# Attention and a two-layer network on one core: the product with the spread reciprocals half as far again behind, and later raw scores in the phases that turn sums

## The chip, the cores and the metric

The kernel runs on one NeuronCore of a Trainium2 chip. The metric is the device time of one execution in microseconds; the time before is the median of three runs. All times are us unless marked ns. PE is the matrix engine (PEld its weight loads), DVE the vector engine, ACT the scalar engine, POOL and SP the two engines that here issue nearly all transfers.

## The reference

Two branches on the same rows, mixed by a gate. Branch a is attention with 32 query heads of width 16 over one shared key and value head; branch b is a two-layer network with a squared ReLU.

```python
g = _sigmoid((x * gate_w).sum(-1, keepdims=True))
...
q = (lambda x, *d: x.transpose(*d))((x @ wq).reshape(B, S, H, Dh), 0, 2, 1, 3)
k = x @ wk
v = x @ wv
scores = jnp.einsum("bhqd,bkd->bhqk", q, k) * (Dh ** -0.5)
p = _softmax(scores, axis=-1)
o = jnp.einsum("bhqk,bkd->bhqd", p, v)
return (lambda x, *d: x.transpose(*d))(o, 0, 2, 1, 3).reshape(B, S, H * Dh) @ wo
...
h = jnp.einsum("bsd,df->bsf", x, w1) + b1
r = jnp.where(h > zero, h, zero)
h = r * r
out = jnp.einsum("bsf,fd->bsd", h, w2) + b2
...
return g * a + (1 - g) * b
```

The arrays are float32, with S 2048, D 512, H 32, Dh 16 and F 1792.

## The kernel before

The queries come in 4 chunks of 512 rows, each with 8 groups of 4 heads. For a group, the scores are made for 16 blocks of 128 keys, in two halves of the queries: 1024 units in all. A unit is four heads by 256 queries for one block of keys: two score matmuls of 512 columns (rows 0 to 63 and 64 to 127 of PE work at once), one exponential of 1024 columns on ACT (line 873), and four context matmuls by the values (line 893) that add into the bank acc. The values carry a column of ones, so that the rows of acc hold sums of exponentials beside the outputs.

PE takes turns. A phase (`phase`, line 1236) makes the scores of 4 to 9 units a few units ahead, mixed with the matmuls M of another piece of work (a span: a query projection, a hidden block of the network, a sum by w2, a projection by wo), and then the context matmuls of units made earlier follow (`context`, line 879). The order in a phase is written out by hand in `PLANS`, by the number of units, of matmuls and the kind of the phase: `S0` is a pair of score matmuls into a bank pair s, which ACT reads itself; `02` and `12` are the two halves of unit 2, which go as raw scores through the single bank x. DVE copies each half out of x (line 857), and ACT takes the exponential from the copy. So PE's next use of x waits for DVE's copy. The second part of a plan is the order of the exponentials. The same bank x also serves, now and then, to sum the squares of queries (line 425), and in the last phases to turn sums by PE (`turn`, line 966, the transposes in line 976), from which DVE reads in lines 981 to 985. A list `late` marks that x was just used in that way by the queries' squares; then a phase of 6 units and 12 matmuls, whole, takes the plan `LATER`, whose raw score comes later.

Engines work through their own queues in order. In which order DVE gets its work is decided while the program is written, by a running estimate of each engine's clock (`at_pe`, `at_dve`, `at_act`): `spend` (line 674) fills the gaps before a raw score is due with waiting jobs: remainders of rounded weights, the list `divisions`, biases, and the list `chores`, which loads and rounds the output weights and the attention outputs (lines 643 and 646; L643 is a cast, L646 its remainder).

After two groups of heads, `finish` (line 929) moves sums and outputs by SP into the tiles lq and oc, and `divide` (line 910) makes the jobs of `divisions`, 15 times: clamp the sums (lines 921, 922), invert them and let POOL send them to memory and back, spread over the rows, into lc (line 916, and the transfers in lines 917 and 918), and multiply oc by lc (line 925). `LAST_OK` is 15, and the number i of the division runs from 0 to 14. A job carries an earliest time: the product's is 24 us (`SPREADS`) behind that of the inversion, 10 us for the last one. Then POOL stores the tile (line 959), and when all tiles of a chunk are stored, `ask` (line 1048) puts its loading and rounding on `chores`, from which the chunk's projection by wo follows.

POOL's queue also holds stores of the rounded weights for reuse (line 521) and, in the first part of the program, stores of the queries' remainders (line 369, 15 of them), whose tiles are later taken over by the hidden block's results (lines 202 and 203).

Of the kernel before, what the change touches and what calls it, by code (L numbers as in the profile page):

```python
# [15 lines left out]
OP = mybir.AluOpType  # L16
# [16 lines left out]
ROOT = float(0x1fbd1df5 + 0x80000)  # L33
WARM = 10
LW = 4 * CH // 64
LANDS, DIVIDES, WRITES, SPREADS, SURE = 6.0, 22.0, 14.0, 24.0, 1.4
PAIR, CONTEXT, TURN, EXP, COPY, LATE = 0.235, 0.429, 0.36, 0.925, 0.66, 0.3
GROUPS = [[(0, 1, 2, 3), (4, 5, 6, 7, 8), (9, 10, 11, 12, 13)]] + [[(0, 1, 2, 3, 4), (5, 6, 7, 8, 9), (10, 11, 12, 13)]] * 3
AHEAD = 4
WHOLE, FIRST, SECOND, LATER = range(4)  # L40
# [7 lines left out]
    (6, 12, WHOLE): ("M 02 S0 M S1 M M M M M S3 M M M S4 12 M M S5", (0, 1, 3, 4, 5, 2)),  # L48
    (6, 12, LATER): ("S0 M M S1 M M M 02 M S3 M M M S4 M 12 M M S5", (0, 1, 3, 4, 5, 2)),
    (6, 9, WHOLE): ("S0 M 03 M S1 M M M S2 M M M S4 13 M S5", (0, 1, 2, 4, 5, 3)),  # L50
    (6, 6, WHOLE): ("S0 M S1 M 03 M S2 M 13 M S4 M S5", (0, 1, 2, 4, 3, 5)),
    (6, 6, SECOND): ("S0 M S1 M 03 M S2 M 13 M S4 M S5", (0, 1, 2, 4, 3, 5)),
    (4, 6, WHOLE): ("M 02 S0 M M S1 M M 12 M S3", (0, 1, 3, 2)),
# [9 lines left out]
LAST_OK = NC * KT - 1  # L63
# [106 lines left out]
def mix_kernel(ctx: ExitStack, tc: tile.TileContext, xT, wkv, wq, wo, w12, b1, b2, cst, out):  # L170
    nc = tc.nc
# [66 lines left out]
    with fast, tc.tile_pool(name="at", bufs=1) as at, \  # L238
# [8 lines left out]
        def aside():  # L247
            return mp.tile([128, CH], F32, name="x", bufs=1)
# [420 lines left out]
        def step_aside():  # L669

            if side and next(side[0], "end") == "end":
                side.pop(0)
# [138 lines left out]
        es, wide = {}, []  # L811
# [98 lines left out]
        def divide(o, l, i, ready):  # L910

            n = at.tile([128, LW], F32, name="n")
            wide = at.tile([128, CH], F32, name="lc", bufs=2)

            def over():
                nc.vector.reciprocal(n, n)
                nc.gpsimd.dma_start(ls[i].rearrange("a (b n) -> (a b) n", b=16), n)
                nc.gpsimd.dma_start(wide, bass.AP(tensor=ls.tensor, offset=ls[i].offset,
                                                  ap=[[CH, 8], [0, 16], [1, CH]]))

            return ((0.1, ready, lambda: nc.vector.tensor_scalar(n, l, L_MIN, L_MAX, op0=OP.max, op1=OP.min)),
                    (0.2, ready, lambda: nc.vector.scalar_tensor_tensor(l, n, 1.0, l, op0=OP.mult, op1=OP.is_equal,
                                                                        accum_out=ok[:, i:i + 1])),
                    (0.3, ready, over),
                    (0.72, ready + (SPREADS if i < LAST_OK - 1 else LANDS + 4.0), lambda: nc.vector.tensor_tensor(o, o, wide, OP.mult)))

        sums = []

# [37 lines left out]
        def turn(a, u, js, okc, idle=0):  # L966

            if not o2:
                o2.append(at.tile([128, 4, 2, 4, DH], F32, name="o2", tag="oc", bufs=2))
            js = slice(js[0], js[-1] + 1)  # L970
            m = js.stop - js.start
            if m > 2:
                yield
            tp = aside().rearrange("p (j n) -> p j n", j=4)
            for j in range(m):
                nc.tensor.transpose(tp[:, j], a[:, j * 128:(j + 1) * 128], ident)
            busy(idle)
            p5 = tp[:, :m].rearrange("p j (h d e) -> p j h d e", h=4, e=2)
            l = p5[:, :, :, 0, 1]
            n = at.tile([128, 2, 4, 4], F32, name="nl")[:, :, :m]  # L980
            nc.vector.tensor_scalar(n[:, 0], l, L_MIN, L_MAX, op0=OP.max, op1=OP.min)
            nc.vector.scalar_tensor_tensor(n[:, 1], n[:, 0], 1.0, l, op0=OP.mult, op1=OP.is_equal,
                                           accum_out=ok[:, okc:okc + 1])
            nc.vector.reciprocal(n[:, 0], n[:, 0])
            nc.vector.tensor_tensor(o2[0][:, js, u], p5[:, :, :, :, 0],
                                    n[:, 0].unsqueeze(3).to_broadcast([128, m, 4, DH]), OP.mult)
# [36 lines left out]
        def busy(n):  # L1023

            if n and not junk:
                junk.append(sp.tile([128, 2, CH], F32, name="s")[:, 0])
            for _ in range(n):
                nc.tensor.matmul(junk[0], cs[:, :64].bitcast(BF), cs[:, :CH // 2].bitcast(BF), start=True, stop=True)
# [207 lines left out]
        def phase(slots, n, m):  # L1236

            nonlocal scored, evicted, at_pe
            if span.done[0] == 0:
                begin()  # L1240
            step_aside()
            kind = SECOND if span.done[0] else WHOLE if slots == span.slots else FIRST
            if late and (n, slots, kind) == (6, 12, WHOLE):
                kind = LATER
            late.clear()
            text, order = PLANS.get((n, slots, kind)) or plain(n, slots)
            rows = [], []
            for item in text.split():
                if item[0] == "0":
                    rows[0].append(item)  # L1250
                elif item[0] == "1":
                    rows[1].append(item)
                else:
                    for r in range(2):
                        rows[r].append(item)
            todo = [scored + i for i in order]

            for i in range(len(rows[0])):
                for r in range(2):
                    item = rows[r][i]  # L1260
                    if item == "M":
                        span.product(r)
                    elif item[0] == "S":
                        score_part(scored + int(item[1:]), r)
                    else:
                        score_copy(scored + int(item[1:]), r)
                    exps(todo)
                at_pe += PAIR
            exps(todo)
            assert not todo  # L1270
            scored += n
            if not span.left():
                evicted = span.before
                if evicted:
                    spend(at_pe + 0.3)
                    dve(0.76, at_pe + 0.3)
                    evicted.unit[1](evicted.bank)
            if not any(item[0] == "0" for item in text.split()):
                spend(at_pe)
            while wanted:  # L1280
                w_load(wanted.pop(0))
            for half in range(2):
                if NF <= len(ws[half]) < min(room[half], NC * NF):
                    w_fetch(half)
            for half in halves():
                if spans > 5 and w_ready(half):
                    if at_act + 0.64 < at_pe + 0.7 + CONTEXT * m:
                        w_round(half, scalar_copy)
                    elif at_dve + 0.6 < at_pe + 0.7 + CONTEXT * m:
                        w_round(half, nc.vector.tensor_copy)  # L1290
# [47 lines left out]
        late, halved, units_left = [], [0.0], [NC * (NF + 12) + 15 + 16]  # L1338
# [11 lines left out]
        while u < total:  # L1350
# [6 lines left out]
            m, slots = block(u)  # L1357
# [59 lines left out]
```

## Time and profile before

| what | us |
|---|---|
| median of three runs (lowest, highest) | 1208.13 (1207.78, 1211.83) |
| the profiled execution | 1204.39 |
| its span, first to last instruction | 1202.6 |
| PE busy | 1180.2 |
| ACT busy | 1025.7 |
| DVE busy | 673.0 |
| mean granted PE clock | 0.994 |

The span is what the profile's rows cover; 1.8 us of the execution lie round it. A row of the timeline gives the start, the duration, the engine, the line, the operation with the tile written and the tiles read, and in brackets how long the engine had been idle before it and what released it. A row of the waits gives who waited for whom: total, times, longest. A group's row gives the count, the busy time, the mean of one in ns and the idle time ahead of its instances.

### The profile page before, as it was taken

To read this page: it belongs to the slowest core of one execution; us is meant where nothing else is said; L and a number is where in the kernel's file an instruction comes from. 1 tells how busy PE (TensorE), PEld (TensorE's weight loads), DVE (VectorE), ACT (ScalarE), POOL (GpSimd) and SP (SyncE) were. 2 spreads that over 40 slices of the span, in tenths; PEclk is the share of its full clock that TensorE was granted. 3 is DMA by queue.
4 is the path that set the end of the run, shared out by engine and by line. 5 is a ranking of instruction groups with operands and counts; after the bars stand their busy time and mean duration, and the time that the engine had idled before them with its cause. 6 is when DMAs were issued, how large, how long until landed. Compare 5 with 4: busy or idle time off the path is not lost.

```text
span 1202.6 us, 32004 instructions
## 1 busy us (share of the span) xinstructions
PE 1180.2 (98%) x13814; PEld 781.0 (65%) x13815; DVE 673.0 (56%) x1110; ACT 1025.7 (85%) x1134; POOL 81.0 (7%) x145
## 2 busy tenths in 40 slices
PE   9999979999999999999999999999999999999996
PEld 4766656666666666666666666666666666666663
DVE  6766657674654744463556644553747447445543
ACT  5789869998988888888888898888888888988873
POOL 1311110010000000100000000000000000000000
PEclk9999989999999999999999999999999999999999
DMA  7556443342353513330444315221424125131111
GB/s 235 184 161 200 125 137 116 108 142 84 120 177 110 173 47 117 104 91 20 131 152 146 117 43 170 77 64 46 154 69 158 48 90 169 37 100 58 51 45 38
DMA packets 54202, 132.71 MB, mean 110 GB/s; under 512 B 14554, under 2 KB 15050, under 8 KB 53544
## 3 DMA queue, kind: packets, MB, share of 16 engines
q1 hardware_dynamic: 37896, 88.70, 23.9%
q0 software_dynamic: 16016, 41.65, 10.2%
q8 instruction: 110, 1.80, 0.6%
q14 instruction: 36, 0.29, 0.1%
q10 hardware_dynamic: 144, 0.26, 0.1%
HBM read 85.88 MB, written 40.09 MB: 105 GB/s over the span
## 4 chain that ended last, share of the span: by engine, by line
PE 87%; issue 8%; DMA 1%; POOL 1%; DVE 1%; ACT 1%; SPq 0%; POOLq 0%; DVEq 0%
PE acc L893 35%; PE mm L1209 30%; PE s L836 17%; PE x L836 4%; POOL qs L369 1%; ACT e L873 1%; DMA lc<-ls 0%; DMA xf<-in_xT 0%; PE mm L310 0%; PE mm L210 0%; DVE e L857 0%; DMA wf<-in_w 0%; PE s L320 0%; POOL xkept L565 0%; POOL w2kept L521 0%
## 5 line engine op out<-in xcount | busy, mean ns | idle before, releaser
L873 ACT ACTIVATE e<-s 128x1024 f32<-128x1024 f32 x764 | 744.2, 1023 | 104.4 <-PE s L836 102.1
L857 DVE COPY e<-x 128x512 f32<-128x512 f32 x520 | 359.6, 692 | 469.9 <-PE x L836 348.1
L893 PE MATMUL acc<-e,v_ext 128*32 128x256 f32 x8192 | 470.6, 381 | 0.0
L836 PE MATMUL s<-qa,k_aug 49*128 49x512 f32 x1528 | 427.0, 414 | 0.1
L893 PEld LDWEIGHTS acc<-e,v_ext 128*32 128x32 f32 x8192 | 252.1, 110 | 190.9 <-issue 38.8
L873 ACT ACTIVATE e<-e 128x1024 f32<-128x1024 f32 x260 | 274.4, 1058 | 28.7 <-DVE e L857 28.6
L836 PEld LDWEIGHTS s<-qa,k_aug 49*128 49x128 f32 x1528 | 221.2, 185 | 100.7 <-ACT e L873 66.3
L1209 PE MATMUL mm<-w2p,hr 64*128 64x512 f32 x1128 | 242.2, 392 | 0.0
L836 PE MATMUL x<-qa,k_aug 49*128 49x512 f32 x520 | 215.3, 414 | 11.1 <-DVE e L857 9.1
L1209 PEld LDWEIGHTS mm<-w2p,hr 64*128 64x128 f32 x1128 | 157.6, 186 | 18.3
L836 PEld LDWEIGHTS x<-qa,k_aug 49*128 49x128 f32 x520 | 95.8, 184 | 44.5 <-DVE e L857 23.3
L1209 PE MATMUL mm<-xragain,w1p 64*128 64x512 f32 x448 | 120.8, 393 | 0.0
L1209 PE MATMUL mm<-xr,w1p 64*128 64x512 f32 x448 | 117.6, 399 | 0.0
L1209 PEld LDWEIGHTS mm<-xragain,w1p 64*128 64x128 f32 x448 | 69.7, 186 | 5.8
L1209 PEld LDWEIGHTS mm<-xr,w1p 64*128 64x128 f32 x448 | 69.4, 190 | 5.9
L1209 PE MATMUL mm<-xlagain,w1p 64*128 64x512 f32 x224 | 67.8, 393 | 0.0
L1209 PE MATMUL mm<-xl,w1p 64*128 64x512 f32 x224 | 66.3, 398 | 0.0
L1209 PE MATMUL mm<-more 64*128 64x512 f32 x216 | 59.5, 392 | 0.0
L723 DVE TENSOR_SCALAR big<-mm,b1t 128x512 f32<-128x512 f32 x56 | 41.6, 743 | 0.5 <-PE mm L1209 0.5
L724 DVE TENSOR_TENSOR big<-big 128x512 f32<-128x512 f32 x56 | 38.8, 692 | 1.9
L1209 PE MATMUL mm<-wor,orr 64*128 64x512 f32 x120 | 38.6, 398 | 0.5 <-DVE ol L1018 0.5
L1209 PE MATMUL mm<-wor,orl 64*128 64x512 f32 x120 | 38.2, 392 | 0.0
(168 smaller groups left out, 812.0 us busy)
## 6 DMA issues: line engine op xcount, KB each, us to landing
w1p<-w1kept SPq DMA_DIRECT2D x42, 512.0 KB
w2p<-w2kept SPq DMA_DIRECT2D x35, 512.0 KB
qa<-qs SPq DMA_DIRECT2D x186, 64.0 KB
w1kept<-w1p POOLq DMA_DIRECT2D x14, 512.0 KB, 4.1
w2kept<-w2p POOLq DMA_DIRECT2D x12, 512.0 KB, 5.3
qs<-qr SPq DMA_DIRECT2D x16, 256.0 KB
ress<-res POOLq DMA_DIRECT2D x4, 1024.0 KB, 4.6
qs<-ql POOLq DMA_DIRECT2D x15, 256.0 KB, 7.8
```

The source lines that it names most:

```text
L369: eng.dma_start(bass.AP(tensor=o.tensor, offset=o.offset, ap=[[KS * 2 * CH, 4], [CH, 2 * DH], [1, CH]]), src.bitcast(F32))
L723: nc.vector.tensor_scalar(h[0], p, b1t[:, f:f + 1], 0.0, op0=OP.add, op1=OP.max)
L724: nc.vector.tensor_tensor(h[0], h[0], h[0], OP.mult)
L836: nc.tensor.matmul(dst.rearrange("p (a n) -> p a n", a=2), k_aug[rows, kt * 128:(kt + 1) * 128], qa[it][rows, :, q * HC:q * HC + HC], star ...
L857: nc.vector.tensor_copy(e_half(u)[:, 2 * r:2 * r + 2], x.rearrange("p (a n) -> p a n", a=2))
L873: nc.scalar.activation(e_half(u), src, AF.Exp, scale=SCALE)
L893: nc.tensor.matmul(accs[q][h * 32:(h + 1) * 32], v_ext[:, kt], es[u][:, h % 2 * 2 + h // 2], start=kt == 0 and it > 0, stop=kt == NK - 1, ...
L1209: nc.tensor.matmul((self.before if r else self).bank, a[p], b[p], start=not r and i == 0, stop=r == 1 and i == len(self.terms[1]) - 1, ski ...
```

## The change

Two parts. First, `SPREADS` goes from 24 to 36: for the divisions 0 to 11 the product's earliest time lies 36 us behind the inversion's. For 12 and 13 it stays at 24, for 14 at 10. Second, `turn` marks `late` too when it uses x, a phase takes the plan `LATER` whenever there is one for its units and matmuls, and two such plans are added.

```diff
-LANDS, DIVIDES, WRITES, SPREADS, SURE = 6.0, 22.0, 14.0, 24.0, 1.4
+LANDS, DIVIDES, WRITES, SPREADS, SURE = 6.0, 22.0, 14.0, 36.0, 1.4
...
+    (6, 9, LATER): ("S0 M M S1 M M S2 03 M M S4 M 13 M M S5", (0, 1, 2, 4, 5, 3)),
+    (4, 5, LATER): ("S0 M M S1 02 M M 12 M S3", (0, 1, 3, 2)),
...
-                    (0.72, ready + (SPREADS if i < LAST_OK - 1 else LANDS + 4.0), lambda: nc.vector.tensor_tensor(o, o, wide, OP.mult)))
+                    (0.72, ready + (SPREADS if i < LAST_OK - 3 else 24.0 if i < LAST_OK - 1 else LANDS + 4.0), lambda: nc.vector.tensor_tensor(o, o, wide, OP.mult)))
...
             if m > 2:
                 yield
+            late.append(True)
             tp = aside().rearrange("p (j n) -> p j n", j=4)
...
-            if late and (n, slots, kind) == (6, 12, WHOLE):
+            if late and (n, slots, LATER) in PLANS:
                 kind = LATER
```

Behind the added lines, the line numbers of the changed kernel are 2 or 3 higher: the copy is L859, the product L927, the matmuls of the other work L1212, the transposes L979.

On DVE, the place of the first product. Before, from the hidden block's remainder (hr) on; w1p is a weight's remainder, wor the cast of the output weights:

```order
L202 CAST hr<-big 128x512
L203 TENSOR_TENSOR hr<-big,hr 128x512
L925 TENSOR_TENSOR oc<-oc,lc 128x512
L857 COPY e<-x 128x512
L519 TENSOR_TENSOR w1p<-stage,w1p 128x512
L857 COPY e<-x 128x512 x3
```

In the changed kernel, from the three copies that end these rows, on into the next phase:

```order
L859 COPY e<-x 128x512 x3
L725 TENSOR_SCALAR big<-mm,b1t 128x512
L726 TENSOR_TENSOR big<-big 128x512
L204 CAST hr<-big 128x512
L205 TENSOR_TENSOR hr<-big,hr 128x512
L859 COPY e<-x 128x512
L645 CAST wor<-stage 128x512
L859 COPY e<-x 128x512
L521 TENSOR_TENSOR w1p<-wf,w1p 128x512
L859 COPY e<-x 128x512
L927 TENSOR_TENSOR oc<-oc,lc 128x512
L859 COPY e<-x 128x512
```

The product has moved from ahead of a phase's first copy to ahead of the last copy of the next phase; there it takes the place of the remainder of wor (L646 of before), which goes some phases later. The products of the divisions 1 to 11 move on in the same way, by one or two phases.

On DVE, the stretch where the product of division 8 stands before, in the projection of the chunk with the number 1 (L227 are its results):

```order
L857 COPY e<-x 128x512 x4
L227 SCALAR_TENSOR_TENSOR big<-mm,g,big 128x512
L857 COPY e<-x 128x512
L925 TENSOR_TENSOR oc<-oc,lc 128x512
L857 COPY e<-x 128x512 x3
L227 SCALAR_TENSOR_TENSOR big<-mm,g,big 128x512
```

In the changed kernel the same stretch holds the casts and remainders of this chunk's attention outputs (orr, orl), and sums by w2 (L748) follow:

```order
L927 TENSOR_TENSOR oc<-oc,lc 128x512
L859 COPY e<-x 128x512
L645 CAST orr<-stage 128x512
L859 COPY e<-x 128x512
L648 TENSOR_TENSOR orl<-stage,orr 128x512
L645 CAST orr<-stage 128x512
L859 COPY e<-x 128x512
L648 TENSOR_TENSOR orl<-stage,orr 128x512
```

Since the chunk's last product comes later, its outputs are loaded and rounded later, and its four pieces of projection follow a sum of the network that they preceded before. From the product of division 12 on, DVE's order is that of before.

On PE, the phase behind the first turning of sums (cs is the identity; s are scores that ACT reads itself, x is the raw score, mm the projection). Before:

```order
L976 MATMUL x<-cs,accs 128x128 x4
L836 MATMUL s<-qa,k_aug 128x512 x2
L1209 MATMUL mm<-wor,orr 128x512
L836 MATMUL x<-qa,k_aug 128x512
L1209 MATMUL mm<-wol,orr 128x512
L836 MATMUL s<-qa,k_aug 128x512 x2
L1209 MATMUL mm<-wor,orl 128x512
L1209 MATMUL mm<-wor,orr 128x512 x2
L1209 MATMUL mm<-wol,orr 128x512 x2
L836 MATMUL s<-qa,k_aug 128x512 x2
```

And in the changed kernel:

```order
L979 MATMUL x<-cs,accs 128x128 x4
L838 MATMUL s<-qa,k_aug 128x512 x2
L1212 MATMUL mm<-wor,orr 128x512
L1212 MATMUL mm<-wol,orr 128x512
L838 MATMUL s<-qa,k_aug 128x512 x2
L1212 MATMUL mm<-wor,orl 128x512
L1212 MATMUL mm<-wor,orr 128x512 x2
L838 MATMUL s<-qa,k_aug 128x512 x2
L838 MATMUL x<-qa,k_aug 128x512
L1212 MATMUL mm<-wol,orr 128x512 x2
```

The raw score has moved from behind the first pair of scores to behind the third, and the second and third pairs come earlier. It is the only phase whose order of kinds changes for this reason; the plan (4, 5, LATER) is taken in no phase.

## The prediction

> **What bounds the kernel now.** I read the page first, then the waits of the whole program, then the stretch round the longest of them. The first rows are the page's busy line, clock line, and the group of the products with the spread reciprocals (count; busy us, mean ns; idle before them).
>
> ```profile
> PE 1180.2 (98%) x13814; PEld 781.0 (65%) x13815; DVE 673.0 (56%) x1110; ACT 1025.7 (85%) x1134; POOL 81.0 (7%) x145
> ...
> PEclk9999989999999999999999999999999999999999
> ...
> L925 DVE TENSOR_TENSOR oc<-oc,lc 128x512 f32<-128x512 f32 x15 | 10.2, 683 | 7.8 <-DMA lc<-ls 7.8
> ```
>
> PE is the bound: 98% of the span, DVE 56%. So moving DVE work is worth nothing in itself; only a wait that reaches PE counts. The clock falls in one slice near the start, the sixth (150 to 180 us). The product's 15 instances wait for their data 7.8 us in all. PE's own waits and the waits of the stretch from 150 to 170 us (total, times, longest):
>
> ```profile
> PE x L836 <- DVE e L857: 9.1, 3, 7.4
> PE x L836 <- DVE o L985: 1.8, 2, 1.1
> ...
> DVE oc L925 <- DMA lc<-ls: 7.8, 1, 7.8
> ```
>
> The 7.8 us are one single wait, and PE's longest is 7.4 us. The timeline shows that they are one event (start, duration; idle before in brackets), on DVE, PE and POOL:
>
> ```profile
> 132.61 0.35 DVE L916 RECIPROCAL n<-n 128x32 f32<-128x32 f32 x1
> ...
> 153.09 0.69 DVE L203 TENSOR_TENSOR hr<-big,hr 128x512 fp32r<-128x512 f32 x1
> 161.56 0.69 DVE L925 TENSOR_TENSOR oc<-oc,lc 128x512 f32<-128x512 f32 x1 [7.77 <-DMA lc<-ls]
> 162.17 0.68 DVE L857 COPY e<-x 128x512 f32<-128x512 f32 x1
> ...
> 162.91 0.79 PE L836 MATMUL x<-qa,k_aug 49*128 49x512 f32 x1 [7.43 <-DVE e L857]
> ...
> 149.05 0.60 POOL L917 DMA_DIRECT2D ls<-n  x1
> 155.76 0.63 POOL L918 DMA_DIRECT2D lc<-ls  x1 [6.11 <-DMA ls<-n]
> 156.41 0.71 POOL L369 DMA_DIRECT2D qs<-ql  x1
> 164.61 0.70 POOL L369 DMA_DIRECT2D qs<-ql  x1 [7.49 <-DVE e L857]
> ```
>
> The first reciprocals are done at 132.96 us, but in POOL's queue they stand behind the queries' stores (L369), and their two transfers are issued only at 149.05 and 155.76. The product stands at the head of DVE's queue from 153.79 and starts at 161.56. Behind it stands the copy that frees the raw scores' bank x, and for that bank PE stands still for 7.43 us. (The releaser named at the store of 164.61 was done long before it; the store starts when the one before it has landed.)
>
> **What the first wait costs.** Granted clock by stretch (length, PE busy, ..., clock, DMA share, GB/s), and the first rows of the score phases and of the context products that end them:
>
> ```profile
> 155.48:158.00 2.52, 0.00 (x1) 0.00 (x0) 0.00 (x0) 1.10 (x2) 1.34 (x2) 0.94 0.43 51
> 158.00:162.91 4.91, 0.00 (x1) 0.00 (x1) 1.35 (x3) 0.00 (x0) 0.00 (x0) 0.50 0.80 234
> 162.91:167.97 5.06, 5.06 (x24) 3.96 (x26) 1.93 (x3) 1.97 (x2) 1.86 (x3) 0.50 0.41 97
> ...
> 168.41:176.22 7.81, 7.81 (x97) 5.62 (x95) 6.76 (x11) 7.42 (x10) 0.54 (x1) 1.00 0.36 117
> ...
> 153.80 0.50 PE L836 MATMUL s<-qa,k_aug 49*128 49x512 f32 x1
> ...
> 168.41 3.23 PE L893 MATMUL acc<-e,v_ext 128*32 128x256 f32 x56
> ...
> 171.57 0.50 PE L836 MATMUL s<-qa,k_aug 49*128 49x512 f32 x1
> ...
> 176.22 3.23 PE L893 MATMUL acc<-e,v_ext 128*32 128x256 f32 x56
> ```
>
> The phase with the wait lasts 168.41 - 153.80 = 14.61 us; the next one, with the same work, 176.22 - 171.57 = 4.65. The wait costs 9.96 us: 7.43 of standing, and 2.53 because PE runs at clock 0.50 until 167.97, 5.06 us after it starts again. The Trainium skill ("TensorE: Matmul & The Clock Gate", Part 1, "What's actually happening") says that an idle window of about 3.4 us halves the clock, and as long a busy one restores it. By that rule, the half clock would cost half of 3.4 to 6.8 us, an estimate of 1.7 to 3.4, and the wait 9.1 to 10.8 in all; the trace's 2.53 and 9.96 lie inside, so the traced ones are used. It also makes a remnant of the wait under some 3 us cost its own length only, and the trace agrees so far that the clock was granted at 0.94 in the first 2.52 us after PE stopped.
>
> **The first product, moved.** By the order of instructions it now stands after the third copy of the next phase, just where before has the remainder of the first output weights (L646). These are the rows of before from that stretch, with the cast of those weights, and the SP queue's loads of them and of the next rows:
>
> ```profile
> 172.74 0.42 DVE L643 CAST wor<-stage 128x512 fp32r<-128x512 f32 x1
> ...
> 174.92 0.69 DVE L857 COPY e<-x 128x512 f32<-128x512 f32 x1
> 175.53 0.68 DVE L646 TENSOR_TENSOR wol<-stage,wor 128x512 fp32r<-128x512 f32 x1
> ...
> 178.82 0.69 DVE L203 TENSOR_TENSOR hr<-big,hr 128x512 fp32r<-128x512 f32 x1
> ...
> 155.99 0.44 SPq L1038 DMA_DIRECT2D stage<-in_wo  x1
> ...
> 163.48 0.33 SPq L487 DMA_DIRECT2D stage<-in_w  x1
> ...
> lc<-ls POOLq DMA_DIRECT2D x1, 256.0 KB, 5.8
> ...
> qs<-ql POOLq DMA_DIRECT2D x1, 256.0 KB, 7.9
> ```
>
> Without the 9.96 us the slot of 175.53 comes at 165.57. POOL's queue up to the spread transfer holds nothing that moves, so the reciprocals land by 161.56 as before: 4.0 us to spare, and all 9.96 us go. What else had those 9.96 us as a cover? Three transfers were on their way through the wait. First, the output weights: loaded by SP at 155.99, cast now at 172.74 - 9.96 = 162.78. Their landing isn't shown; by the nearest, POOL's two transfers beside them (5.8 and 7.9 us), it is 161.8 to 163.9, so the cast waits 0 to 1.1 us, and PE no longer. I take 0, since they are first in SP's queue. Second, the query store of 156.41 lands at 164.3, and the remainder that overwrites its source (L203) comes at 178.82 - 9.96 = 168.86. Third, the load of 163.48 moves up to about 157, and stands behind the output weights in its queue. It is the one new neighbour of the spread transfer: 256 KB at the 234 GB/s of that stretch are 1.1 us, an estimate, and even wholly added to the landing they leave 2.9 of the 4.0. The Trainium skill ("DMA: Bandwidth & Descriptors", "Queues, rings and completion order") speaks against me here: each DMA engine takes packets of its queues in turn, so an earlier load on SP's queue would slow POOL's transfer. By that rule too the cost is bounded by the load's own 1.1 us, and no run here shows the sharing by itself.
>
> **The other products.** 14 of 15 wait for nothing in before. Eleven more now come later, each 0.68 us of DVE at another place. Their stores on POOL (L959) go with them, the first past two stores of weights; who reads them, the projection of the chunk, asks for them only after the chunk's last product, and for its last two pairs after two pairs have been converted. I count nothing for the stores. What the products cost at their new places lies between -0.4 and 14.0 us: PE's waits for copies beside the two longest are 9.1 - 7.4 - 1.3 = 0.4 in all, which is the most that could go; and the dearest product of before is this one, close to the end, where DVE was behind:
>
> ```profile
> 1137.79 0.68 DVE L925 TENSOR_TENSOR oc<-oc,lc 128x512 f32<-128x512 f32 x1
> ...
> 1137.93 0.50 PE L836 MATMUL x<-qa,k_aug 49*128 49x512 f32 x1 [1.27 <-DVE e L857]
> ```
>
> Eleven times 1.27 are 14.0. I take 0, by the row of the group: 14 places chosen by the same rules cost nothing but that one. The projection of the second chunk now follows a sum instead of preceding it; PE's instructions are the same in number, and its weights are fetched phases ahead. I take 0 for that also.
>
> **The phase after the turned sums.** Rows of before on PE and ACT round the first of the three turnings, the one whose next phase has a new plan:
>
> ```profile
> 1157.76 0.50 PE L836 MATMUL s<-qa,k_aug 49*128 49x512 f32 x2
> ...
> 1159.15 0.47 PE L836 MATMUL x<-qa,k_aug 49*128 49x512 f32 x1 [0.66 <-DVE o L985]
> ...
> 1159.46 0.39 PE L1209 MATMUL mm<-wol,orr 64*128 64x512 f32 x1
> ...
> 1159.69 0.39 PE L836 MATMUL s<-qa,k_aug 49*128 49x512 f32 x1
> ...
> 1162.63 2.80 PE L893 MATMUL acc<-e,v_ext 128*32 128x256 f32 x48
> ...
> 1158.37 1.03 ACT L873 ACTIVATE e<-s 128x1024 f32<-128x1024 f32 x1 [0.97 <-PE s L836]
> ```
>
> PE waits 0.66 us for DVE to read the turned sums out of the bank. With the raw score six places later that wait goes. What is late next is the third score, which needs the bank of the first: its exponential ends at 1158.37 + 1.03 = 1159.40, and its new place, six steps of 0.23 us (1159.46 to 1159.69) after 1157.76, is 1159.14. So 0.26 of the 0.66 come back; I take a gain of 0.4, with bounds of -0.3 (the later exponentials slip too) and 0.7. The other wait of 1.1 us comes in a phase for which there is no late plan, and the plan of four scores over five steps is in no phase that the order shows: nothing for either.
>
> **Sum.** 9.96 + 0.4 = 10.4 us. The profiled execution took 1204.39 us (1202.6 of span and 1.8 round it), so 1194.0 in its terms. Its time is 3.7 us below the median of the runs, 1208.13. If that is a constant, the changed kernel's median is 1208.13 - 10.4 = 1197.7 us.
>
> **Rivals.**
> *The wait of the timed runs is longer.* If the 3.7 us are a spread transfer that lands later, at 165.3, the product at 165.57 still meets it, and 14.1 us go: 1194.0. For it: this wait is the one part of the run that depends on a late queue. Against: no row shows it.
> *Part of the wait is passed on.* The cast 1.1 us, the tail -0.3 instead of 0.4, and two products like that of 1137.79: 1.1 + 0.7 + 2.5 = 4.3, 1202.0. Or the next user of POOL's late stores becomes the one that waits. Against: each had 4 us to spare.
> *The change doesn't do what it says.* The spread transfer slips with the product, by over 4.0 us, and each further us comes back: at 14 us later, 1207.7. Against: its queue on POOL has nothing new ahead of it.
> *Slower.* The places of the later products are bad ones: DVE is behind there, the copy comes late, and PE waits as at 1137.93. Twelve times 1.27 are 15.2: 1208.13 - 10.4 + 15.2 = 1213.0. It decides from 10.4 / 12 = 0.87 us each. Against: one such place among 15.
>
> **Chances and range.** The forecast, within 2 us, 0.66; the longer wait 0.11; part passed on 0.13; no effect 0.05; slower 0.05. A measurement of this kernel can tell about 0.5%, 6 us, from no change. Faster by more than that: 0.88 (the first two and nearly all of the third); within it 0.07; slower 0.05. The range goes from the first rival's 1194.0 to the second's 1202.0; the two cases left out hold 0.10, the edges of the others some more.
>
> **What would show it.** Right: the product's idle time 7.8 becomes 0, PE's longest wait for a copy is the 1.3 us near the end, the clock row has no 8 in its sixth slice, the phase there lasts 4.65 us. For the tail: no wait of 0.66 behind the four turnings, and the phase, 4.87 us before (1157.76 to 1162.63), 4.5. Wrong: a DVE wait for the output weights or for a query store between 160 and 177 us; new waits of PE for copies beside the later products; or the product's wait still in the list.

## The result, and the profile after

The changed kernel takes **1197.34 us** (median of six runs, 1193.26 to 1198.68); the kernel before, beside it on the same chip, 1207.95 (six runs, 1204.67 to 1212.85). The ratio is 0.9898, with a 95% interval from 0.9869 to 0.9928: 10.6 us faster. The forecast was 1197.7. (Ratios, here and below, are formed from runs in the faster of the kernel's two states alone, so they can differ a little from the quotient of two medians.)

The page of the changed kernel, busy line and clock line, and from the list of all groups that of the product with the spread reciprocals (L927 here, L925 before):

```profile
PE 1180.3 (99%) x13814; PEld 782.2 (65%) x13815; DVE 672.9 (56%) x1110; ACT 1025.2 (86%) x1134; POOL 81.1 (7%) x145
...
PEclk9999999999999999999999999999999999999999
...
L927 DVE TENSOR_TENSOR oc<-oc,lc 128x512 f32<-128x512 f32 x15 | 10.2, 681 | 0.0
```

PE's work is the same to 0.1 us; the product's idle time has gone from 7.8 to 0.0, and the clock line has no 8 any more. PE's waits of the whole program (total, times, longest), and the only one of DVE for an output weight:

```profile
PE s L838 <- ACT e L875: 3.0, 1, 3.0
PE x L838 <- DVE e L859: 1.7, 2, 1.3
...
PE x L838 <- DVE o L988: 1.1, 1, 1.1
...
DVE wor L645 <- DMA stage<-in_wo: 0.2, 1, 0.2
```

The 7.4 us at the head of this list before are gone, and so are the 0.66 behind the turned sums. A wait of 3.0 us is new. First the stretch of the moved product in the timeline:

```profile
137.72 0.35 DVE L918 RECIPROCAL n<-n 128x32 f32<-128x32 f32 x1
...
152.42 0.79 POOL L919 DMA_DIRECT2D ls<-n  x1
...
158.93 0.50 PE L838 MATMUL s<-qa,k_aug 49*128 49x512 f32 x1
...
161.96 0.63 POOL L920 DMA_DIRECT2D lc<-ls  x1 [8.75 <-DMA ls<-n]
...
162.81 0.44 SPq L1041 DMA_DIRECT2D stage<-in_wo  x1
...
163.53 3.23 PE L895 MATMUL acc<-e,v_ext 128*32 128x256 f32 x56
...
168.18 0.43 DVE L645 CAST wor<-stage 128x512 fp32r<-128x512 f32 x1 [0.23 <-DMA stage<-in_wo]
...
170.64 0.68 DVE L927 TENSOR_TENSOR oc<-oc,lc 128x512 f32<-128x512 f32 x1
```

The phase lasts 163.53 - 158.93 = 4.60 us; before it lasted 14.61. The transfer of lc is issued at 161.96 and, by the list of transfers for this stretch, lands 3.7 us later: 5.0 us ahead of the product.

Yet the two profiled executions are only 1204.39 - 1198.49 = 5.90 us apart. To see where the rest went, I set the starts of the context matmuls in the two timelines side by side, in the order of the program (138 starts). Their difference moves in steps:

| start, us in before | what | step, us |
|---|---|---|
| 96 to 104 | the same program in both | +5.1 |
| 168.41 | the phase of the first product | -10.0 |
| 564 and 1132 | the same program in both | -0.35 and -0.33 |
| 760 to 842 | projection of the second chunk behind a sum | +7.6, and back |
| 1162.63 | the phase behind the turned sums | -0.48 |

The first row is the new wait. Rows of before, and then of the changed kernel, round the cast of a weight on ACT (L525, L527 after):

```profile
88.28 0.95 SPq L487 DMA_DIRECT2D stage<-in_w  x2
...
100.15 0.63 ACT L525 ACTIVATE w2p<-stage 128x512 fp32r<-128x512 f32 x1 [0.88 <-DMA stage<-in_w]
```

```profile
91.00 2.76 SPq L489 DMA_DIRECT2D stage<-in_w  x2
...
103.71 0.63 ACT L527 ACTIVATE w2p<-stage 128x512 fp32r<-128x512 f32 x1 [3.94 <-DMA stage<-in_w]
...
105.31 0.80 PE L838 MATMUL s<-qa,k_aug 49*128 49x512 f32 x2 [2.95 <-ACT e L875]
```

Up to there both programs are the same (the two steps of a third of a us stand in other_queue below too, and the first of them in first_alone, whose programs differ from before in one place only); SP issued this load 2.7 us later in this execution, and the exponential that PE needs stood behind the cast. It is a difference between executions, not of the change. So two profiles side by side give the change's own part only by their steps: -10.0 and -0.48.

### The profile page after: what moved, and what is told of

Same layout as the page of the kernel before. It is cut to its first block, busy times and chain, and to the rows that moved or that the text cites. A ratio compares the mean times of both kernels' runs of the same rounds, so it can differ in the third digit from the quotient of the medians.

```text
span 1196.7 us, 31998 instructions
## 1 busy us (share of the span) xinstructions
PE 1180.3 (99%) x13814; PEld 782.2 (65%) x13815; DVE 672.9 (56%) x1110; ACT 1025.2 (86%) x1134; POOL 81.1 (7%) x145
## 4 chain that ended last, share of the span: by engine, by line
PE 96%; DMA 1%; DVE 1%; ACT 1%; issue 1%; SPq 0%; DVEq 0%; ACTq 0%
PE acc L895 38%; PE mm L1212 32%; PE s L838 18%; PE x L838 5%; DMA stage<-in_w 1%; ACT e L875 1%; PE mm L312 1%; PE acc L556 0%; PE mm L212 0%; DMA wf<-in_w 0%; PE s L322 0%; DVE e L859 0%; DVE ot L1383 0%; PE x L979 0%; PE mm L322 0%
## 5 line engine op out<-in xcount | busy, mean ns | idle before, releaser
L859 DVE COPY e<-x 128x512 f32<-128x512 f32 x520 | 359.5, 691 | 470.0 <-PE x L838 337.8
L1212 PE MATMUL mm<-w2p,hr 64*128 64x512 f32 x1128 | 242.5, 392 | 0.0
L1212 PEld LDWEIGHTS mm<-w2p,hr 64*128 64x128 f32 x1128 | 157.8, 186 | 18.2
L1212 PE MATMUL mm<-xragain,w1p 64*128 64x512 f32 x448 | 120.7, 393 | 0.0
L838 PEld LDWEIGHTS x<-qa,k_aug 49*128 49x128 f32 x520 | 95.6, 184 | 34.3 <-DVE e L859 14.1
L1212 PE MATMUL mm<-xr,w1p 64*128 64x512 f32 x448 | 116.4, 393 | 0.0
L1212 PEld LDWEIGHTS mm<-xragain,w1p 64*128 64x128 f32 x448 | 69.9, 186 | 5.6
L1212 PEld LDWEIGHTS mm<-xr,w1p 64*128 64x128 f32 x448 | 68.5, 186 | 5.4
L1212 PE MATMUL mm<-xlagain,w1p 64*128 64x512 f32 x224 | 67.8, 393 | 0.0
L1212 PE MATMUL mm<-xl,w1p 64*128 64x512 f32 x224 | 65.6, 391 | 0.0
L1212 PE MATMUL mm<-more 64*128 64x512 f32 x216 | 59.4, 392 | 0.0
L1212 PE MATMUL mm<-wor,orr 64*128 64x512 f32 x120 | 38.4, 399 | 0.5 <-DVE ol L1021 0.5
L1212 PE MATMUL mm<-wor,orl 64*128 64x512 f32 x120 | 38.5, 392 | 0.0
```

The source lines that it names most:

```text
L838: nc.tensor.matmul(dst.rearrange("p (a n) -> p a n", a=2), k_aug[rows, kt * 128:(kt + 1) * 128], qa[it][rows, :, q * HC:q * HC + HC], star ...
L859: nc.vector.tensor_copy(e_half(u)[:, 2 * r:2 * r + 2], x.rearrange("p (a n) -> p a n", a=2))
L1212: nc.tensor.matmul((self.before if r else self).bank, a[p], b[p], start=not r and i == 0, stop=r == 1 and i == len(self.terms[1]) - 1, ski ...
```

## The experiments

My theory: the first product, at the head of DVE's queue, costs all of the gain, since PE stands behind it and then runs at half clock; the late transfer comes from POOL's queue; the other edits are worth nothing or 0.4. The rivals: the other products or the projection matter too; part of the wait is passed on to the next load; or the transfer itself is slow. The table has all runs; steps are against the one profile of before, as above, the second figure those of the next two phases.

| kernel | median (lowest to highest, runs) | ratio, 95% interval | step at 168.41 |
|---|---|---|---|
| first_alone | 1198.56 (1194.0 to 1207.33, 12) | 0.9944, 0.9919 to 0.9968 | -9.98 |
| all_but_first | 1206.22 (1201.27 to 1214.79, 12) | 1.0002, 0.9974 to 1.0029 | -0.28 |
| behind_two_copies | 1212.52 (1) | one execution | -1.01, then +2.74 |
| behind_three_copies | 1205.96 (1) | one execution | -9.99, then +6.41 |
| other_queue | 1196.34 (1194.65 to 1200.4, 8) | 0.9917, 0.9883 to 0.9952 | -9.98, then +2.26 |
| later_casts | 1202.71 (1194.18 to 1206.74, 12) | 0.9949, 0.9916 to 0.9983 | -9.98, then +3.10 and +1.54 |
| changed_again | 1199.92 (1194.3 to 1203.75, 11) | 0.9923, 0.9894 to 0.9951 | -9.97, then +1.60 and +0.16 |
| wor_cast_later | 1195.82 (1193.3 to 1202.44, 10) | 0.9906, 0.9876 to 0.9936 | -9.94 |
| remainders_by_sp | 1207.83 (1202.86 to 1213.1, 12) | 1.0008, 0.9981 to 1.0034 | -9.98, then +0.74 |
| both_moved | 1208.3 (1203.81 to 1217.37, 12) | 1.0031, 0.9998 to 1.0063 | -9.99 |
| wor_cast_later_again | 1197.21 (1194.65 to 1206.25, 8) | 0.9905, 0.9866 to 0.9944 | -9.99, then 0 and +1.15 |
| changed_beside | 1197.89 (1194.69 to 1205.96, 7) | 0.9898, 0.9874 to 0.9922 | -9.98, then +0.17 and +1.22 |

The kernel before took 1206.06 us beside the first four, 1208.94 beside the next three, 1208.57 beside the three after, and 1209.73 beside the last two; single runs of it went from 1195.35 to 1222.58.

**The first product alone, and all but it.**

```diff
 # first_alone: before, with
-ready + (SPREADS if i < LAST_OK - 1 else LANDS + 4.0)
+ready + (36.0 if i == 0 else SPREADS if i < LAST_OK - 1 else LANDS + 4.0)
 # all_but_first: the changed kernel, with
-ready + (SPREADS if i < LAST_OK - 3 else 24.0 if i < LAST_OK - 1 else LANDS + 4.0)
+ready + (24.0 if i == 0 else SPREADS if i < LAST_OK - 3 else 24.0 if i < LAST_OK - 1 else LANDS + 4.0)
```

> The kernel before with one edit: the product of division 0 alone goes from 24 to 36 us behind its inversion. Theory (the wait of the first product is the gain): the phase of that product lasts about 4.6 us instead of 14.6, no wait for lc, and the time falls by 10.0 us against before, ratio 0.992, all of the changed kernel's gain but about 0.4 us. Rival (the gain is spread over the twelve moved products, or lies in the plan behind the turned sums): the phase still waits, or the ratio is above 0.996.

> The changed kernel with the product of division 0 back at 24 us: divisions 1 to 11 moved, and the later raw score behind the turned sums. Theory: the wait of 7 to 8 us and the half clock are back, the later products cost nothing, the tail gives 0.4 to 0.5 us; ratio 0.9996 against before, between 0.997 and 1.002. Rival (the later products carry part of the gain): ratio below 0.996. Rival (their new places are bad ones, 0.87 us or more each): ratio above 1.005.

Waits of PE and of the product in all_but_first:

```profile
PE x L838 <- DVE e L859: 8.4, 3, 6.8
DVE oc L927 <- DMA lc<-ls: 7.1, 1, 7.1
```

The wait is where it was (7.1 us instead of 7.8), the step at 168.41 is only -0.28, and the ratio is 1.0002. What remains of the change shows as a step of -0.48 at 1162.63, which that measurement can't tell from nothing. With the first product alone, the step is -9.98 and there is none at 1162.63. Both sides of the theory hold. By its medians, first_alone gained 7.5 us and not 10, and its ratio of 0.9944 lies between the 0.992 of the theory and the 0.996 of the rival. Its interval overlaps that of every run of the changed kernel, so this does not show a second gain; what speaks against one is all_but_first.

**Moved by less.** SPREADS is 26 and 28 for the first division in the kernel before, so that the product stands behind two or three copies of its phase instead of none.

```diff
-ready + (SPREADS if i < LAST_OK - 1 else LANDS + 4.0)
+ready + (26.0 if i == 0 else SPREADS if i < LAST_OK - 1 else LANDS + 4.0)   # 28.0
```

> The kernel before with the product of division 0 at 26 us: in DVE's order it stands behind two more raw-score copies, so that DVE reaches it about 2.7 us later. Theory: DVE still waits 4 to 5 us for lc; PE, which stops later than before, waits 3.7 to 4.8 us for the bank x, and its clock still falls to half about 2.5 us after it stops, so that the phase costs 1 to 2.5 us more than the wait; that stretch lasts 5 to 7 us longer than without a wait, instead of 10. Rival (the half clock comes from something else than PE's standing, say the transfers): the clock stays at 1.00, or the surplus over the wait is 2.5 us as before whatever the wait.

> The kernel before with the product of division 0 at 28 us: in DVE's order behind three more copies, ahead of the last of the phase. Theory: DVE waits 2.5 to 4 us for lc, but the context products go on meanwhile; PE waits 0.2 to 1.2 us for x, its clock stays at 1.00, and of the 10.0 us 8.8 to 9.8 go. Rival (any wait of DVE there costs PE as much): the stretch lasts 2.5 to 4 us longer than without a wait.

Rows of DVE, PE and POOL, first behind two copies, then behind three, and from the latter the clock in stretches (length, PE busy, ..., clock, DMA share, GB/s):

```profile
165.71 0.62 POOL L918 DMA_DIRECT2D lc<-ls  x1 [6.23 <-DMA ls<-n]
...
171.66 0.69 DVE L925 TENSOR_TENSOR oc<-oc,lc 128x512 f32<-128x512 f32 x1 [8.89 <-DMA lc<-ls]
...
173.01 0.79 PE L836 MATMUL x<-qa,k_aug 49*128 49x512 f32 x1 [8.40 <-DVE e L857]
```

```profile
162.44 0.63 POOL L918 DMA_DIRECT2D lc<-ls  x1 [6.14 <-DMA ls<-n]
...
168.93 0.69 DVE L925 TENSOR_TENSOR oc<-oc,lc 128x512 f32<-128x512 f32 x1 [5.93 <-DMA lc<-ls]
...
170.28 0.79 PE L836 MATMUL x<-qa,k_aug 49*128 49x512 f32 x1 [3.06 <-DVE e L857]
...
167.22:170.28 3.06, 0.00 (x1) 0.00 (x1) 1.35 (x3) 0.02 (x1) 0.00 (x0) 0.78 0.55 176
170.28:175.00 4.72, 4.60 (x17) 2.89 (x19) 3.96 (x8) 4.57 (x6) 2.07 (x3) 0.50 0.22 31
175.00:176.00 1.00, 1.00 (x8) 0.84 (x6) 0.68 (x2) 0.26 (x1) 0.02 (x1) 0.62 0.88 299
```

Both sizes were missed, for two reasons. The transfer came later than in the profile of before (counted from the end of the reciprocals, lc was issued 22.8 us after it in before, 26.4 and 24.3 here), so both waits were longer than expected. And a stand of 3.06 us cost 5.8: PE then ran at clock 0.50 for another 5.5 us. What was confirmed is the direction: behind the third copy PE stands for 3.06 of the product's 5.93 us, since it has its context matmuls left, and behind two copies it stands for nearly all of it. Both executions also ran at clock 0.50 for 13.65 us from 26 us on, with PE busy nearly all the time as far as its rows show; that put about 5 us on their totals, which the steps leave out. So the clock can also fall without a stand of PE, and no run shows why it did there.

**The queue.** The kernel before at its 24 us, with the first division's two transfers on SP.

```diff
-nc.gpsimd.dma_start(ls[i]...)
-nc.gpsimd.dma_start(wide, ...)
+(nc.sync if i == 0 else nc.gpsimd).dma_start(ls[i]...)
+(nc.sync if i == 0 else nc.gpsimd).dma_start(wide, ...)
```

> The kernel before with its distance of 24 us; only the first division's two transfers of reciprocals are issued by SP instead of POOL, so that no store of the queries' remainders stands ahead of them. If POOL's queue makes the wait: DVE does not wait for lc, the phase behind it lasts 4.6 us instead of 14.6, and the median comes to 10 us below before, near 1196 to 1198. If the transfer itself is slow, or DVE's own order is at fault, the wait stays within 2 us of 7 to 8 and the time is that of before. If SP, held up for the first transfer's landing, delays the loads of queries behind it, the wait goes but others come in for it: a wait of PE or ACT for qa between 145 and 165 us, and less than 8 us are won.

```profile
132.22 0.35 DVE L916 RECIPROCAL n<-n 128x32 f32<-128x32 f32 x1
132.60 0.35 SPq L917 DMA_DIRECT2D ls<-n  x1
...
139.23 0.65 SPq L918 DMA_DIRECT2D lc<-ls  x1
...
153.32 0.68 DVE L925 TENSOR_TENSOR oc<-oc,lc 128x512 f32<-128x512 f32 x1
...
165.14 0.51 DVE L643 CAST wor<-stage 128x512 fp32r<-128x512 f32 x1 [2.67 <-DMA stage<-in_wo]
...
166.30 0.49 PE L836 MATMUL x<-qa,k_aug 49*128 49x512 f32 x1 [1.83 <-DVE e L857]
```

With the product left where it was, its wait is gone all the same: lc is issued 6.7 us behind the reciprocals instead of 22.8. So the distance was short because of the stores in POOL's queue, and the step is again -9.98. The run remainders_by_sp below shows the same from the other side: there the two transfers stay on POOL and the stores leave it, and lc is issued 6.2 us behind the reciprocals and lands 13.2 us behind them, instead of 28.6. The Trainium skill ("DMA: Bandwidth & Descriptors", "Issuing engines are not separate DMA queues") says that moving transfers among the issuing engines gives no bandwidth, since they share the same DMA engines; that fits what was won here, which is a place in an order and not a faster transfer (from the first issue to the second it took 6.63 us on SP, and 6.71 on POOL in before). But the next phase shows what I had priced at nothing: the output weights' cast now waits 2.67 us for its load, and PE 1.83. By the steps, 7.7 us are won in the two phases together; by the ratio 10.0, with an interval from 5.8 to 14.1. So the third branch (less than 8 us, since another wait comes in) is not excluded, though the wait that came is for the weights and not for qa.

**The casts near 100 us.** In the changed kernel, in the first 16 spans, a weight's cast on ACT comes 18 instead of 12 us of the planner's clock behind its load; beside it the changed kernel again.

```diff
-and at_pe - since[half][n] > 2 * LANDS)
+and at_pe - since[half][n] > (2 if spans > 16 else 3) * LANDS)
```

> The changed kernel; in the first 16 spans a weight's cast on ACT is placed one estimated landing later behind its load (18 instead of 12 us of the planner's clock). If the cast that waits up to 5.8 us for its load near 100 us is what sets the profiles of one kernel apart there: ACT has no wait for the stage of in_w over 1 us near 100 us, PE none for an exponential over 1 us, and the median is 2 to 5 us below the changed kernel's on the same chip, about 1193 to 1195. If that wait only stands in profiled executions, or the later casts make the next load or remainder late in their turn, the medians agree within 2 us; if the sums by these weights have to wait, it is slower.

> The changed kernel itself, beside later_casts on the same chip: 1195 to 1199 and a ratio of 0.990 if the gain holds; in its profile no wait for lc, and near 100 us a wait of the cast for its load of 0 to 6 us.

From 100 to 140 us of later_casts there is no wait for that load, but its median is 2.8 us above changed_again's, with intervals that overlap: no gain. Its profile waits elsewhere: DVE waits 2.54 us at 146.46 for a store of the queries' remainders, and 3.54 us at 168.54 for the output weights. Changed_again, whose 1199.92 us are a little above what I expected, has a wait at another place of the early part:

```profile
118.48 0.69 DVE L408 CAST qr<-mm 128x512 fp32r<-128x512 f32 x1 [4.76 <-DMA qs<-ql]
...
120.54 0.59 PE L427 MATMUL x<-sq,blk 128*32 128x512 bf16 x1 [4.19 <-DVE sq L412]
...
168.86 0.44 SPq L1041 DMA_DIRECT2D stage<-in_wo  x1
...
170.11 0.62 POOL L920 DMA_DIRECT2D lc<-ls  x1 [6.50 <-DMA ls<-n]
...
173.98 0.43 DVE L645 CAST wor<-stage 128x512 fp32r<-128x512 f32 x1 [2.12 <-DMA stage<-in_wo]
176.66 0.69 DVE L927 TENSOR_TENSOR oc<-oc,lc 128x512 f32<-128x512 f32 x1 [0.38 <-DMA lc<-ls]
```

A tile of the queries was not yet stored when it was needed again: POOL's queue once more. In that queue lc, too, came so late that even the moved product waited 0.38 us, where I had expected no wait.

**The stores, and the output weights' cast.** Two edits of the changed kernel, alone and together.

```diff
 # wor_cast_later
-                    return WRITES
+                    return 20.0
 # remainders_by_sp
-def q_write(c, t, qr, ql, second=nc.gpsimd):
+def q_write(c, t, qr, ql, second=nc.sync):
```

> The changed kernel; the cast of the output weights stands 20 instead of 14 us of the planner's clock behind their load, so one phase later on DVE. If the 0.2 to 3.5 us that DVE waits for these weights in the profiles with the first product moved are a wait that the change took over from the product's (which covered the load before), there is no wait for the stage of in_wo in this profile, no step behind the phase of the moved product, and the median is 1 to 3 us below the changed kernel's. If that wait hides in PE's lead of work, the median is that of the changed kernel within 1 us (1197 to 1200 over the runs so far).

> The changed kernel; the 15 stores of the queries' remainders are issued by SP, right behind the queries' own stores, instead of by POOL. If POOL's queue, in which each store waits for the one ahead to land, is what makes lc late and the tiles of the remainders come free late: the transfer of lc is issued about 10 us earlier than in the changed kernel and lands over 10 us ahead of the product, DVE waits for no store of ql, and the median is 2 to 6 us below the changed kernel's, with less scatter. If SP's own queue is no faster, the loads behind these stores (queries, weights) come late: new waits of PE for qa or of ACT and DVE for stage, and the time is that of the changed kernel or up to 10 us above.

> Both of the two edits above in the changed kernel. If each takes away its own wait, the gains add up: 3 to 8 us below the changed kernel, 1190 to 1195, and no wait of DVE over 1 us for a transfer between 95 and 185 us. If they have one cause (SP's late issue of both loads and stores), the sum is that of the better one alone.

Rows of remainders_by_sp on SP, POOL, DVE, ACT and PE:

```profile
94.47 1.94 SPq L489 DMA_DIRECT2D stage<-in_w  x2
...
106.27 0.63 ACT L527 ACTIVATE w2p<-stage 128x512 fp32r<-128x512 f32 x1 [4.71 <-DMA stage<-in_w]
...
107.86 0.50 PE L838 MATMUL s<-qa,k_aug 49*128 49x512 f32 x2 [3.72 <-ACT e L875]
...
146.88 0.64 POOL L920 DMA_DIRECT2D lc<-ls  x1 [5.26 <-DMA ls<-n]
...
174.01 0.68 DVE L927 TENSOR_TENSOR oc<-oc,lc 128x512 f32<-128x512 f32 x1
```

POOL is free, lc is issued 27 us ahead of its product, and no tile of remainders is late. Still the whole gain of the change is gone (1207.83 and 1208.3): SP now issues the load near 100 us at 94.47 (93.52 in both_moved), and the cast waits 4.71 (5.72). The load was issued at 88.28 in before, where the cast waited 0.88, and at 91.00 in the changed kernel, where it waited 3.94. In these profiles, then, each queue has a short place of its own. But the time of issue is not all: in all_but_first the load was issued at 88.83, and the cast waited 5.17. Nor do the traces account for the whole loss: the steps near 100 us add up to +7.4 in remainders_by_sp, against +5.1 in the changed kernel's own profile, while the medians lie about 10 us apart. That the longer wait is in most timed executions of the two kernels is inferred from their medians; only one of each was traced. The time of both_moved fits neither of its branches, since it is no better than the worse of the two edits.

The later cast of the output weights takes away its wait (none in the profiles of wor_cast_later and its repetition). To see what that is worth, it ran once more beside the changed kernel:

> The changed kernel with the later cast of the output weights once more, now beside the changed kernel on the same chip. If that cast's wait costs time in most executions: 1 to 4 us below the changed kernel beside it. If what sets executions apart is the stretch near 100 us: the medians agree within 1.5 us, and both spread over 1193 to 1203.

> The changed kernel, to be compared with the run above: 1196 to 1200, ratio near 0.991. If the wait for the output weights matters, some wait of 1 to 3.5 us for the stage of in_wo stands in its profile; if not, under 0.5.

1197.21 against 1197.89: no difference, as the second branch said, and the 0.67 us for the weights in changed_beside lie between the two cases that I had named. The largest waits of that profile are others: DVE waited 3.54 and 4.44 us (at 109.14 and 138.21) for stores of the queries' remainders in POOL's queue, and PE stood for 2.00 and 2.88 us behind them. The waits for lc, in wor_cast_later_again and then in changed_beside, which also waited for the weights:

```profile
167.98 0.69 DVE L927 TENSOR_TENSOR oc<-oc,lc 128x512 f32<-128x512 f32 x1 [1.37 <-DMA lc<-ls]
```

```profile
169.85 0.63 POOL L920 DMA_DIRECT2D lc<-ls  x1 [5.64 <-DMA ls<-n]
...
173.26 0.43 DVE L645 CAST wor<-stage 128x512 fp32r<-128x512 f32 x1 [0.67 <-DMA stage<-in_wo]
...
177.01 0.69 DVE L927 TENSOR_TENSOR oc<-oc,lc 128x512 f32<-128x512 f32 x1 [1.44 <-DMA lc<-ls]
```

No version here beats the changed kernel by more than can be measured.

## Why the prediction was right, point by point

**The first product: 9.96 us predicted, 9.94 to 10.00 measured**, in all ten profiles in which it stands late or its transfer goes by SP, and 0.28 where it is put back. The mechanism is shown from three sides: the place alone (first_alone), the rest alone (all_but_first), and the queue alone (other_queue, and lc's landing in remainders_by_sp).

**The margin of 4.0 us was not a constant.** I had the transfer land as in the one profile. Counted from the end of the reciprocals, lc landed after 161.56 - 132.96 = 28.6 us in before and 27.6 in the changed kernel, but after 34.9 in changed_again (170.11 + 6.5 by its list of transfers - 141.69), and after 35.5 in changed_beside: 8 us of scatter, which is more than the margin. The product then waited 0.38 and 1.44 us, and the steps of that phase, +0.16 and +1.22, show that most of the longer wait reached PE. So in such an execution even 36 us are a little short.

**The output weights' cast: 0 taken, 0 to 1.1 as bounds; 0.23, 2.12 and 0.67 measured** in three profiles of the changed kernel, up to 3.54 in later_casts. The bound failed, and not for a late landing: where the cast waits, its start is the landing, and counted from the issue by SP (162.81, 168.86 and 169.32) this load landed after 5.4, 5.1 and 3.9 us, sooner than the 5.8 to 7.9 that I took. What I had wrong is the issue. I kept the 6.8 us that lay between issue and cast by the rows of before (162.78 - 155.99), and in the three profiles the cast's place was only 5.1, 3.0 and 3.3 us behind it. (In other_queue the landing was late as well, 9.0 us behind the issue.) That PE waits no longer than the cast held: the steps of that phase are 0, +1.60 and +0.17, and +2.26 behind the 2.67 of other_queue. But the 0 that I took was wrong. So part of the wait is passed on in some executions, as that rival said, with up to 1.8 us for the two waits together in a profile of the changed kernel. Against 10.5 this is small, and the median forecast without it was not off by it.

**The other products and the projection: 0, and it is 0.** PE's waits for copies are 1.7 us in all, against 9.1 - 7.4 = 1.7 before; the detour of +7.6 at the second chunk's projection comes back to within 0.1; all_but_first measures a ratio of 1.0002.

**The phase behind the turned sums: 0.4, measured 0.48.** The timeline of the changed kernel:

```profile
1151.80 0.66 PE L979 MATMUL x<-cs,accs 128*128 128x128 f32 x4
1152.38 0.50 PE L838 MATMUL s<-qa,k_aug 49*128 49x512 f32 x2
...
1154.07 0.50 PE L838 MATMUL s<-qa,k_aug 49*128 49x512 f32 x2
1154.40 0.39 PE L838 MATMUL x<-qa,k_aug 49*128 49x512 f32 x1
...
1156.77 2.80 PE L895 MATMUL acc<-e,v_ext 128*32 128x256 f32 x48
```

The phase lasts 1156.77 - 1152.38 = 4.39 us, 4.87 before, and the raw score at 1154.40 waits for nothing. The third pair of scores is late as forecast: it starts 1154.07 - 1152.38 = 1.69 us after the first, where the bank of the first was to be free at 1159.40 - 1157.76 = 1.64.

**"A remnant of the wait under some 3 us costs its own length only": this step failed.** The runs gave stands of PE of several lengths. Behind each, the time at clock 0.50 follows from the granted clock of the stretches, and the cost is the stand and half of what was run at 0.50 (the steps of the last two rows are counted from a phase without the wait, 10.0 below before):

| kernel, start of the stand | PE stood | clock 0.50 in all | of it while PE ran | cost | step |
|---|---|---|---|---|---|
| other_queue, 164.5 | 1.83 | 0 | 0 | 1.8 | 2.3 |
| later_casts, 146.6 | 1.92 | 0 | 0 | 1.9 | 2.3 |
| changed_beside, 107.9 | 2.00 | 3.4 | 3.4 | 3.7 | 3.9 |
| later_casts, 167.0 | 2.62 | 3.4 | 3.4 | 4.3 | 4.6 |
| changed_beside, 136.1 | 2.88 | 3.4 | 3.1 | 4.5 | 3.9 |
| changed, 102.4 | 2.95 | 3.4 | 3.4 | 4.6 | 5.1 |
| behind_three_copies, 167.2 | 3.06 | 6.9 | 5.5 | 5.8 | 6.4 |
| remainders_by_sp, 104.1 | 3.72 | 3.4 | 3.4 | 5.4 | 5.4 |
| wor_cast_later, 94.1 | 3.73 | 6.9 | 6.1 | 6.8 | 6.8 |
| changed_again, 116.4 | 4.19 | 6.8 | 5.3 | 6.9 | 7.0 |
| before, 155.5 | 7.43 | 10.2 | 5.0 | 10.0 | 10.0 |
| behind_two_copies, 164.6 | 8.40 | 10.2 | 6.4 | 11.6 | 11.7 |

Three stands left out of the table agree: 4.10 and 6.81 us in all_but_first and 4.73 in both_moved cost 5.8, 9.8 and 6.7, with steps of 5.8, 9.7 and 6.8. From 2.0 us on, a stand cost 1.3 to 1.9 times its length. The row of before that I had taken for agreement says the opposite: a mean clock of 0.94 over 2.52 us is 0.3 us at 0.50, so the clock had fallen 2.2 us after PE stopped. For the forecast it did no harm, since no remnant was left in the phase of the product; for the two runs with the product behind two and three copies it did.

**The constant of 3.7 us.** I carried the distance of the profiled execution to the median over. It was -1.2 for the changed kernel's profile (1197.34 - 1198.49), because of the early wait. The medians differ by 10.6, and the steps of the traces by 10.5: the sum was right, not the constant. That the median came within 0.4 us of the forecast is luck in part: the interval of the ratio spans a gain of 8.7 to 15.8 us, and the two later runs of the changed kernel lie 9.0 and 11.8 us below before. The longer wait of the timed runs (14.1 us) is not what the median shows; that single runs of before spread over 27 us fits the scatter of lc and of the early loads, but which of them made which run was not traced.

## What to carry to other kernels

When a helper's transfer waits in a queue behind other stores, read its landing from several executions before giving a margin: here it moved by 8 us, twice the margin that one profile showed. A short stand of PE is dearer than it looks, so price it with the half clock behind it, from some 2 us on. And compare two profiles by steps at common landmarks: the totals here said 5.9 us, the steps 10.5.

## What the hardware showed beside this

The half clock came in pieces of 3.4, 6.9 and 10.2 us, that is once, twice or three times 3.41 (four times in the early stretch of two profiles), and not in proportion to the stand. It began 1.7 us after PE stopped in behind_three_copies, 2.2 in before and 4.6 in behind_two_copies; in later_casts only 1.7 us after PE had started again.

What the falls have in common is seen when each trace is cut into windows of 3.41 us that fit the places where its clock changes. Between 30 and 1160 us, the clock fell behind 13 such windows in the 14 profiles, and in these PE stood for 1.7 to 3.4 us; in no window behind which it stayed at 1.00 did PE stand for more than 1.33. Rows of later_casts, and then one of other_queue (length, PE busy, ..., clock, DMA share, GB/s):

```profile
167.91:171.32 3.41, 1.70 (x13) 1.24 (x13) 2.78 (x5) 1.24 (x2) 0.00 (x0) 1.00 0.88 244
171.32:174.73 3.41, 3.41 (x34) 1.58 (x36) 3.31 (x7) 3.32 (x4) 1.65 (x3) 0.50 0.40 110
```

```profile
162.38:165.79 3.41, 2.08 (x19) 1.49 (x15) 0.74 (x3) 2.55 (x3) 1.66 (x3) 1.00 0.25 82
```

In the first window PE stands for 1.71 us, and the next one runs at 0.50. In other_queue the stand of 1.83 us reaches over two windows, with 1.33 us of it in this one, and the clock stays at 1.00. In the last 40 us, where short stands follow one another, this does not tell the cases apart: the clock fell behind windows with 1.0 to 1.8 us of standing and stayed behind others with up to 1.9.

The Trainium skill ("TensorE: Matmul & The Clock Gate", Part 1, "What's actually happening") tells of a free-running window of 3413 ns, and the pieces agree with it. By it, a whole idle window would be needed, and its section "Why this matters for your kernels" warns of gaps of some 3 us; here a stand of 2.00 us did it in changed_beside, and in the last window before the half clock of behind_three_copies PE stood for only 1.7 of 3.4 us. Where between 1.33 and 1.71 us of one window the bound lies, and what else counts near the end, these runs don't settle.
